# Linear attention and a gated feed-forward in one kernel: the first q tile is loaded and normalised alone, by head halves, and the last output tile is made by columns

## The chip, the cores and the metric

The kernel runs on one core of a Trainium2 chip. The metric is the device time of one execution in microseconds, the median over several runs. The core has a matrix engine (TensorE; PE in the profile, with its weight loads as PEld), a vector engine (VectorE, DVE), a scalar engine (ScalarE, ACT), GpSimd (POOL) and SyncE (SP). SP computes nothing here; it issues most of the DMAs. Each engine works through its own list of instructions in order, and semaphores hold an instruction back until what it needs is there.

## The reference

Eight batches of eight heads, with 576 positions and 64 channels a head, go through linear attention with a cosine weighting. The result is regrouped to 4608 tokens of 512 channels, normalised by its root mean square, and sent through a gated feed-forward of width 1536.

```python
theta = np.pi / 2.0 * pos / S
phi = lambda x: concat([relu(x) * cos(theta), relu(x) * sin(theta)])      # 64 -> 128 channels
kv  = einsum('bhsf,bhsd->bhfd', phi(k), v)          # 128 x 64 for each head
z   = sum over s of phi(k)
num = einsum('bhsf,bhfd->bhsd', phi(q), kv);  den = phi(q) . z + 1e-06
x   = (num / den)  as  [B * S, H * D] = [4608, 512]
xn  = x / sqrt(mean(x * x) + 1e-06) * rms_g
out = (silu(xn @ w_gate) * (xn @ w_val)) @ w_out    # 512 -> 1536 -> 512
```

Inputs and output are float32. The kernel multiplies in bfloat16 and accumulates in float32.

## The kernel before

**Tiles.** The 576 positions of a batch are four tiles of 128 (number c or j; position 4p + j lies on partition p) and a tail of 64. The tails of two batches make one more tile of 128, so there are nine feed-forward blocks of 512 tokens: one for each batch, and block 8 from the eight tails.

**From q, k, v to a token tile.** `k_phi` and `q_phi` make one half each (cosine or sine) of phi for one tile, on DVE or ACT. `v_cast` brings v to bfloat16. `kvz_pe` (in the opening `kvz_half`) multiplies phi(k) and v for each head, 5 matmuls a head, and v carries a column of ones, so z comes along; `kvz_evac` copies the result out of PSUM. phi(q) has to be transposed: in batches 0 and 1 by PE (`q_tr_pe`, then a copy `q_tr_evac`), later by a DMA on SP's queue (`q_tr_dma`). `nd_pe` multiplies it with kv, one matmul a head, and `nd_post` divides by the denominator on DVE (three instructions: add, reciprocal, multiply). `x_sq` takes the sum of squares on ACT and the power of -1/2 on POOL (`rs`), `x_norm` scales on DVE with `gb`, the norm's weights, and the tile is transposed again: `x_tr_pe` and `x_tr_evac` in batches 0 and 1, `x_tr_dma` on SP's queue later.

**The feed-forward.** A block has 12 steps n. `gval_step` makes the gate and the value of 128 hidden channels for 512 tokens (four matmuls of 512 columns into psG, four into psV), then silu on ACT and the product on DVE. Four `out_step`s follow, one for each tile j, of 12 matmuls each, with a copy out of PSUM and a store.

**What sets the order.** The list of every engine is written out by hand. After batch 0, the work on the next batches is put into slots: `at(block, n, where, ...)` hangs it to step n of a block (12 to 15 are the four `out_step`s), `pe` ahead of the step's matmuls, `pre` after them and ahead of silu or the store, `post` at the end. In the opening, block 0 is made in pieces by `open_ffn` as its token tiles come (steps 0 to 5; 128 or 256 columns at a time), and `filler` puts matmuls on zeros between them. The second layer of block 0 (`out_mm`, lines 712 to 737) goes step by step through n for all four tiles at once, with the work of batch 1 in between.

**Queues.** SP issues loads, transposes and stores in program order. Its DMAs use eight semaphores in turn, so each also waits until the eighth before it has landed. POOL issues the weights, which are converted to bfloat16 on the way: `gval_slice` makes one DMA each for w_gate (wg) and w_val (wv), for hidden channels 0 to 256, 256 to 768 and 768 to 1536. The first of them waits for the first half of v. Steps 0 and 1 need the first pair, steps 2 to 5 the second, steps 6 to 11 the third. The loads of batch 1 on SP wait for the third wg (line 614), and the four DMAs of w_out (wo, three steps n each) on POOL wait for q of batch 1 (line 627). The q tails, with batch 2 behind them, wait for the third quarter of wo (line 723).

**The opening's loads on SP** (lines 121 to 137): k heads 0 to 3, k heads 4 to 7, tiles 0 and 1 of q (one DMA), v heads 0 to 3, 4 and 5, 6 and 7, tiles 2 and 3 of q, `gb`. ACT issues the tails of k and v.

Of the kernel before, what the change touches and what calls it, by code (L numbers as in the profile page):

```python
# [9 lines left out]
FP32 = mybir.dt.float32  # L10
# [12 lines left out]
def kernel(  # L23
# [37 lines left out]
    psO = ps_open.tile([P, 2, 512], FP32, name="psO")  # L61

# [44 lines left out]
    def load_pair(which, b, jj, queue=nc.sync, heads=(0, 8)):  # L107

        key = (which, b)
        if key not in raw:  # L110
            raw[key] = one.tile([P, H, 4 * D], FP32, name=f"r{which}", tag=f"r{which}")
        view = src_of[which][b, :, 0:512, :].rearrange("h (p j) d -> p h j d", j=4)
        return queue.dma_start(
            out=raw[key][:, heads[0] : heads[1], jj * 2 * D : (jj + 1) * 2 * D],
            in_=view[:, heads[0] : heads[1], 2 * jj : 2 * jj + 2, :].rearrange(
                "p h j d -> p h (j d)"
            ),
        )
# [6 lines left out]
    load_pair("q", 0, 0)  # L125
    first["v"] = load_main("v", v, 0, LOW)
    load_main("v", v, 0, (4, 6))
    load_main("v", v, 0, (6, 8))
    load_pair("q", 0, 1)
# [213 lines left out]

    x_of = {}
    state = {"x": 0}
    rs_of = {}

    def nd_post(b, j, pst):
        o = headview(pst)
        xt = xts[state["x"] % NXT]  # L350
        state["x"] += 1
        rec = four.tile([P, 2, 4], FP32, name="rec", tag="rec")
        nc.vector.tensor_scalar(
            out=rec[:, :, :], in0=o[:, :, :, D], scalar1=1e-6, scalar2=None, op0=ALU.add
        )
        nc.vector.reciprocal(out=rec[:, :, :], in_=rec[:, :, :])
        nc.vector.tensor_tensor(  # L357
            out=xt[:, 0:DM].rearrange("p (b h d) -> p b h d", b=2, d=D),
            in0=o[:, :, :, 0:D],
            in1=rec[:, :, :].unsqueeze(3).to_broadcast([P, 2, 4, D]),  # L360
            op=ALU.mult,
        )
        x_of[(b, j)] = xt
# [100 lines left out]
    pairs = [(psG[0], psV[0]), (psG[1], psV[1]), (psO, psO)]  # L464
    filler(26, idle)
# [8 lines left out]
    def gval_slice(c0, c1):  # L474
# [5 lines left out]
        weight_dmas[0].ins, first["v"].ins.name, SYNC_DEP, reason="weights after v"  # L480
# [3 lines left out]
    for c in (0, 1):  # L484
        q_phi(V, 0, c, 0)
        q_phi(A, 0, c, 1)
    for c in (0, 1):
        bank = (psG[1] if c == 0 else psV[1])[:, :]
        q_tr_pe(0, c, bank)
        filler(3, idle)  # L490
        q_tr_evac(V, 0, c, bank)
    v_cast(A, 0, LOW)
    v_cast_tail(A, 0)
    filler(2, idle)
# [4 lines left out]
    filler(1, idle)  # L499
    v_cast(V, 0, (4, 6))  # L500
    v_cast(V, 0, (6, 7))
    v_cast(A, 0, (7, 8))
    kvz_half(0, half_view[1], range(4, 6))
    filler(1, idle)
    kvz_half(0, half_view[1], range(6, 8))
    filler(2, idle)
    kvz_half_evac(A, 0, half_view[0], 0)
    kvz_half_evac(V, 0, half_view[1], 1)
    for c in (2, 3):
        q_phi(A, 0, c, 1)  # L510
    nd_pe(0, 0, psA)
    nd_pe(0, 1, psO)
    nd_post(0, 0, psA)
    x_sq(0, 0)
    nd_post(0, 1, psO)
    x_sq(0, 1)
    filler(10, idle)
    q_phi(V, 0, 2, 0)
    x_norm(0, 0)
    q_phi(V, 0, 3, 0)  # L520

    def open_ffn(pair, steps, c0, c1, base=0):

        x = xnT[0]
        for i, n in enumerate(steps):
            for a, w in ((0, wg), (1, wv)):
                bank = pairs[pair][a]
                bank = bank[:, a, :] if pair == 2 else bank[:, :]
                lo = base + 256 * i + c0 % 256
                for t in range(NDT):  # L530
                    nc.tensor.matmul(  # L531
                        bank[:, lo : lo + c1 - c0],
                        lhsT=w[:, t, n * P : (n + 1) * P], rhs=x[:, t, c0:c1],
                        start=(t == 0), stop=(t == NDT - 1),
                    )

    def open_h(pair, n, half):
        if 0 not in hTs:
            hTs[0] = two.tile([P, NNT, TB], BF16, name="hT", tag="hT")
        g, v_ = (  # L540
            pairs[pair][a][:, a, :] if pair == 2 else pairs[pair][a][:, :] for a in range(2)
        )
# [9 lines left out]
    q_tr_pe(0, 2, psO[:, 0, :])  # L552
    q_tr_evac(A, 0, 2, psO[:, 0, :])
    x_tr_pe(0, 0, psG[1][:, :])
    x_tr_evac(V, 0, 0, psG[1][:, :])
    x_norm(0, 1)
    filler(1, idle)
    open_ffn(0, (0, 1), 0, 128)
    x_tr_pe(0, 1, psG[1][:, :])
    x_tr_evac(V, 0, 1, psG[1][:, :])  # L560
    q_tr_pe(0, 3, psO[:, 1, :])
    q_tr_evac(A, 0, 3, psO[:, 1, :])
    nd_pe(0, 2, psA)
    nd_post(0, 2, psA)
    open_ffn(0, (0, 1), 128, 256)
    nd_pe(0, 3, psA)
    nd_post(0, 3, psA)
    x_sq(0, 2)
    open_ffn(1, (2, 3), 0, 256)
# [40 lines left out]
    wo_dmas = []  # L610

    def first_loads_of_1():
        d = load_main("k", k, 1, bufs=two)
        tc.add_manual_dep(d.ins, weight_dmas[4].ins.name, SYNC_DEP, reason="after the weights")
        load_tail("k", k, 1)
        gate = load_main("q", q, 1)
        load_main("v", v, 1, LOW)
        load_main("v", v, 1, HIGH)
        load_tail("v", v, 1)
        for i in range(4):  # L620
            d = nc.gpsimd.dma_start(
                out=wo[:, 3 * i : 3 * i + 3, :],
                in_=moe_w_out[3 * i * P : 3 * (i + 1) * P, :].rearrange("(t p) m -> p t m", p=P),
            )
            wo_dmas.append(d)
            if i == 0:
                tc.add_manual_dep(d.ins, gate.ins.name, SYNC_DEP, reason="after batch 1")

    first_loads_of_1()


    for c in range(5):
        at(0, 7 + c // 3, "post", k_phi, V, 1, c, 0)
        at(0, 7 + c // 3, "post", k_phi, A, 1, c, 1)
    for c in range(4):
        at(0, 9 + c // 2, "post", q_phi, V, 1, c, 0)
        at(0, 9 + c // 2, "post", q_phi, A, 1, c, 1)
    at(0, 11, "post", v_cast, A, 1, LOW)
    at(0, 11, "post", v_cast, V, 1, HIGH)
# [3 lines left out]
    for nb in range(2, B):  # L643
# [10 lines left out]
        vb, vn = (b, 2) if late else (b - 1, 14)  # L654
# [7 lines left out]
        for j in range(4):  # L662
            n = nds[j]
            at(b, n, "pe", nd_pe, nb, j, psA)
            at(b, n, "pre", nd_post, nb, j, psA)
            at(b, n, "post", x_sq, nb, j)
            at(b, n + 1, "post", x_norm, nb, j)
            at(b, n + 1, "post", x_tr_dma, nb, j)
# [38 lines left out]
    def tr1(j):  # L707
        x_tr_pe(1, j, psV[j % 2][:, :])
        x_tr_evac(A, 1, j, psV[j % 2][:, :])

    qbank = [psA[:, 0, :], psV[0][:, :], psV[1][:, :], psA[:, 0, :]]
    for n in range(NNT):
        for c in ((0, 1), (2,), (3,))[n] if n < 3 else ():
            q_tr_pe(1, c, qbank[c])
            q_tr_evac(V if c % 2 else A, 1, c, qbank[c])
        if n == 3:
# [10 lines left out]
        if n in (7, 9, 11):  # L727
            x_norm(1, n // 2 - 3)
        if n in (4, 6, 8, 10):
            j = n // 2 - 2  # L730
# [3 lines left out]
        if n in (9, 11):  # L734
            tr1(n // 2 - 4)
        for j in (2, 3, 0, 1) if n == NNT - 1 else range(4):
            out_mm(0, j, n, banks0[j])
    out_store(A, 0, 2, banks0[2])
    out_store(V, 0, 3, banks0[3])
    tr1(2)  # L740
# [3 lines left out]
    for n in range(2):  # L744
        gval_mm(1, n, n, (0, 256))
    x_tr_pe(1, 3, psC[0][:, :])
    x_tr_evac(A, 1, 3, psC[0][:, :])
# [16 lines left out]
    for blk in range(1, 9):  # L764
        for n in range(2 if blk == 1 else 0, NNT):
            gval_step(blk, n)
        for j in range(4):
            out_step(blk, j)

# [29 lines left out]
```

## Time and profile before

| | |
|---|---|
| median of 6 runs | 337.5 us (335.79 to 339.81) |
| profiled execution: its time, its span | 338.65 us, 336.9 us |
| PE busy | 321.7 us, 96% of the span |
| of it on zeros (`filler`, 49 matmuls) | 13.7 us |
| DVE, ACT busy | 180.6 us, 169.5 us |
| first feed-forward matmul | at 20.21 us |
| step 6 of block 0, first `out_mm` | at 32.92 us, at 45.00 us |
| first matmul of block 2 | at 100.22 us |
| last copy out of PSUM begins | at 332.24 us |

Times inside an execution count from the first instruction. The span ends with the last instruction; 1.75 us of the execution's time lie around it. PE is the engine with the most work, so what counts is where it waits, where it works on zeros, and what it waits for. A wait is put down to the engine or the DMA whose signal came last.

### The profile page before, as it was taken

The numbers are of one execution on the slowest core, as the hardware profiler recorded it, in microseconds if no ns is written. First come the engines' busy times: TensorE is split into PE (matmuls) and PEld (weight loads), VectorE is DVE, ScalarE is ACT, GpSimd is POOL, SyncE is SP. The second block draws the span as 40 slices with busy tenths as digits, with TensorE's granted clock in tenths as the row PEclk, the third lists the DMA queues.
The fourth block names the chain that finished last, engine by engine and source line by source line (L and its number), as shares of the span: only waits on it lengthen the run. The fifth ranks groups of instructions, "written<-read, shape, count | busy, mean of one in ns | idle before, by whom it ended". The sixth has DMA issues, their size and how long they took to land.

```text
span 336.9 us, 5945 instructions
## 1 busy us (share of the span) xinstructions
PE 321.7 (96%) x2193; PEld 163.3 (48%) x2193; DVE 180.6 (54%) x372; ACT 169.5 (50%) x327; POOL 37.5 (11%) x83
## 2 busy tenths in 40 slices
PE   8789999899959999999999999999999999999994
PEld 3569455544424544454455445544544444444441
DVE  3675747577824676467446764674567334203410
ACT  5655853775625456644564566455654233223321
POOL 3520311101100012001100120011001000000000
PEclk9999999999998999999999999999999999999999
DMA  8999999968696977797769678877552310030014
GB/s 206 283 207 264 275 187 254 328 152 191 151 248 129 199 180 201 180 205 178 221 152 219 166 215 157 204 191 226 126 74 44 105 54 0 2 120 5 2 31 94
DMA packets 94957, 54.14 MB, mean 161 GB/s; under 512 B 59984, under 2 KB 90192, under 8 KB 94928
## 3 DMA queue, kind: packets, MB, share of 16 engines
q1 hardware_dynamic: 89072, 48.78, 57.6%
q0 software_dynamic: 4768, 4.72, 8.5%
q10 hardware_dynamic: 1088, 0.26, 0.4%
q8 instruction: 17, 0.28, 0.4%
q14 instruction: 12, 0.10, 0.1%
HBM read 38.01 MB, written 9.44 MB: 141 GB/s over the span
## 4 chain that ended last, share of the span: by engine, by line
PE 81%; DMA 9%; SPq 3%; DVE 2%; ACT 2%; issue 1%; POOL 0%; DVEq 0%; ACTq 0%
PE psC L440 24%; PE psG L420 24%; PE psV L420 24%; DMA rq<-in_q_dram 6%; PE psA L303 2%; PE psA L331 2%; SPq L86 2%; DMA wo<-in_moe_w_out_dram 2%; DMA out_dram<-osb 1%; PE psG L460 1%; DVE xt L357 1%; PE psG L531 1%; PE psV L531 1%; PE psO L531 1%; SPq L75 1%
## 5 line engine op out<-in xcount | busy, mean ns | idle before, releaser
L435 DVE TENSOR_TENSOR hT<-psV,sg 128x512 bf16<-128x512 f32 x102 | 70.4, 690 | 103.9 <-PE psV L420 90.4
L420 PE MATMUL psG<-xnT,wg 128*128 128x512 bf16 (+1 forms) x368 | 93.6, 377 | 4.9 <-DMA rq<-in_q_dram 3.5
L429 ACT ACTIVATE sg<-psG 128x512 f32<-128x512 f32 x102 | 60.6, 594 | 69.1 <-PE psG L420 69.0
L420 PE MATMUL psV<-xnT,wv 128*128 128x512 bf16 (+1 forms) x368 | 93.6, 377 | 0.0
L440 PE MATMUL psC<-wo,hT 128*128 128x512 bf16 x408 | 92.0, 379 | 0.7 <-DMA wo<-in_moe_w_out_dram 0.7
L440 PEld LDWEIGHTS <-hT 128*128 128x128 bf16 x432 | 41.2, 98 | 48.5 <-DMA wo<-in_moe_w_out_dram 0.8
L420 PEld LDWEIGHTS <-wv 128*128 128x128 bf16 x416 | 40.9, 98 | 48.0 <-issue 1.1
L420 PEld LDWEIGHTS <-wg 128*128 128x128 bf16 x416 | 38.9, 98 | 46.1 <-issue 6.5
L275 ACT COPY osb<-psC 128x512 f32<-128x512 f32 x33 | 19.3, 586 | 46.4 <-PE psC L440 46.4
L374 POOL TENSOR_TENSOR rs<-ms,mhalf 128x1 f32<-128x1 f32 x36 | 19.9, 554 | 202.4 <-ACT scr L369 202.4
L369 ACT ACTIVATE scr<-xt 128x513 bf16<-128x513 f32 x36 | 22.9, 635 | 25.9 <-DVE xt L357 25.1
L381 DVE SCALAR_TENSOR_TENSOR xn<-xt,rs,gb 128x512 bf16<-128x512 f32 x36 | 27.3, 757 | 15.2 <-POOL rs L374 15.2
L357 DVE TENSOR_TENSOR xt<-psA,rec 128x512 f32<-128x512 f32 x35 | 24.2, 691 | 1.2
L216 ACT ACTIVATE qp<-rq,tab 128x512 bf16<-128x512 f32 x32 | 22.2, 713 | 1.7 <-DMA rq<-in_q_dram 1.7
L216 ACT ACTIVATE kpm<-rk,tab 128x512 bf16<-128x512 f32 (+1 forms) x34 | 21.2, 675 | 0.4 <-DMA rk<-in_k_dram 0.4
L218 DVE TENSOR_SCALAR kpm<-rk,tab 128x512 bf16<-128x512 f32 (+1 forms) x38 | 15.2, 451 | 4.1 <-ACT tab L171 3.1
L331 PEld LDWEIGHTS <-qpT 128*128 128x128 bf16 x256 | 12.2, 98 | 7.8 <-issue 0.6
L218 DVE TENSOR_SCALAR qp<-rq,tab 128x512 bf16<-128x512 f32 x32 | 15.2, 487 | 0.6 <-DMA rq<-in_q_dram 0.6
L460 PE MATMUL psG<-warm 128*128 128x512 bf16 x49 | 13.7, 424 | 1.2 <-DVE fidx L153 1.2
L331 PE MATMUL psA<-kvzs,qpT 128*128 128x65 bf16 x248 | 13.1, 193 | 0.4 <-DVE xt L357 0.3
L420 PE MATMUL psG<-xnt_tail,wg 128*128 128x512 bf16 x48 | 12.3, 379 | 0.0
L420 PE MATMUL psV<-xnt_tail,wv 128*128 128x512 bf16 x48 | 12.3, 379 | 0.0
(90 smaller groups left out, 189.9 us busy)
## 6 DMA issues: line engine op xcount, KB each, us to landing
out_dram<-osb SPq DMA_DIRECT2D x32, 256.0 KB, 2.8
rv<-in_v_dram SPq DMA_DIRECT2D x22, 256.0 KB, 3.2
rk<-in_k_dram SPq DMA_DIRECT2D x20, 256.0 KB, 3.4
rq<-in_q_dram SPq DMA_DIRECT2D x20, 256.0 KB, 3.2
rk<-in_k_dram SPq DMA_DIRECT2D x2, 1024.0 KB, 7.7
rq<-in_q_dram SPq DMA_DIRECT2D x2, 1024.0 KB, 8.6
rv<-in_v_dram SPq DMA_DIRECT2D x3, 512.0 KB, 9.2
wo<-in_moe_w_out_dram POOLq DMA_DIRECT2D x4, 384.0 KB, 7.4
```

The costliest lines, as they stand in the source:

```text
L216: nc.scalar.activation(out=out_ap, in_=in_ap, func=AF.Relu, scale=scale)
L218: eng.tensor_scalar(out=out_ap, in0=in_ap, scalar1=scale, scalar2=0.0, op0=ALU.mult, op1=ALU.max)
L275: nc.scalar.copy(out=o, in_=i)
L331: nc.tensor.matmul(o[:, g, i, :], lhsT=qpT[(b, 0)][:, h, j * P : (j + 1) * P], rhs=kvzs[(b, g)][:, i * E : (i + 1) * E], start=True, stop= ...
L357: nc.vector.tensor_tensor(out=xt[:, 0:DM].rearrange("p (b h d) -> p b h d", b=2, d=D), in0=o[:, :, :, 0:D], in1=rec[:, :, :].unsqueeze(3). ...
L369: nc.scalar.activation(out=scr[:, :], in_=xt[:, 0 : DM + 1], func=AF.Square, scale=1.0 / math.sqrt(DM), accum_out=ms[:, :],)
L374: nc.gpsimd.tensor_tensor(out=rs[:, :], in0=ms[:, :], in1=mhalf[:, :], op=ALU.pow)
L381: nc.vector.scalar_tensor_tensor(out=xn[:, :], in0=x_of[(b, j)][:, 0:DM], scalar=rs_of[(b, j)][:, :], in1=gb[:, :], op0=ALU.mult, op1=ALU. ...
L420: nc.tensor.matmul(pst[bank][:, cols[0] : cols[1]], lhsT=w[:, t, n * P : (n + 1) * P], rhs=x[:, t, cols[0] : cols[1]], start=(t == 0), sto ...
L429: nc.scalar.activation(out=sg[:, :], in_=psG[bank][:, :], func=AF.Silu)
L435: nc.vector.tensor_tensor(out=hTs[blk][:, n, :], in0=psV[bank][:, :], in1=sg[:, :], op=ALU.mult)
L440: nc.tensor.matmul(bank, lhsT=hTs[blk][:, n, j * P : (j + 1) * P], rhs=wo[:, n, :], start=(n == 0), stop=(n == NNT - 1),)
```

## The change

The first q load brings tile 0 alone, then v, then tile 1 alone, and tiles 2 and 3 together. The first weight DMA waits for that first q load in place of the first half of v. The first quarter of wo is issued on POOL right behind the weights; the other three wait for the first half of v of batch 1 in place of q.

In the opening, tile 0 of q is transposed alone. Its `nd_pe` and `nd_post` are done by head halves, each in its own bank (psO is now two tiles). Tile 1 follows after it. `open_ffn` for steps 2 and 3 now runs in two pieces of 128 columns, the first right behind that of steps 0 and 1 and ahead of tile 1's transposes; before, it ran once with 256 columns behind `nd_pe(0, 3)`. ACT and DVE share the copies in another way, and there are 43 fillers for 49.

In block 0, phi of batch 1 sits one step later, and its last q tile and its cast of v move into the second layer. Batch 1's tiles sit at steps 4, 6, 8, 9 of it for 4, 6, 8, 10, and its last two steps are done pair by pair. In block 1 the cast of batch 2's v sits one step earlier. `x_norm` and `x_tr_dma` in slots 12 and later go to `pre`, ahead of that step's store. The last tile of block 8 is made in two halves of 256 columns in two banks, each copied and stored by itself, by SP and ACT.

```diff
-    load_pair("q", 0, 0)
-    first["v"] = load_main("v", v, 0, LOW)
+    first["q"] = load_tokens("q", 0, 0, 1)
+    load_main("v", v, 0, LOW)
     load_main("v", v, 0, (4, 6))
     load_main("v", v, 0, (6, 8))
-    load_pair("q", 0, 1)
+    load_tokens("q", 0, 1, 2)
+    load_tokens("q", 0, 2, 4)
...
-        weight_dmas[0].ins, first["v"].ins.name, SYNC_DEP, reason="weights after v"
+        weight_dmas[0].ins, first["q"].ins.name, SYNC_DEP, reason="weights after q"
...
+    wo_load(0)
+    q_phi(V, 0, 0, 0)
+    q_phi(A, 0, 0, 1)
+    q_tr_pe(0, 0, psV[0][:, :])
+    q_tr_evac(V, 0, 0, psV[0][:, :])
+    filler(4, idle)
+    v_cast(A, 0, (0, 2))
+    v_cast(V, 0, (2, 4))
+    v_cast_tail(V, 0)
...
+    q_phi(V, 0, 1, 0)
+    nd_half(0, 0, 0, psO[0])
+    nd_post_half(0, 0, 0, psO[0])
+    q_phi(A, 0, 1, 1)
+    nd_half(0, 0, 1, psO[1])
+    nd_post_half(0, 0, 1, psO[1])
+    x_sq(0, 0)
...
     q_phi(V, 0, 2, 0)
     x_norm(0, 0)
+    q_tr_pe(0, 2, psO[0][:, :])
+    filler(2, idle)
+    nd_post(0, 1, psA)
     q_phi(V, 0, 3, 0)
...
     x_tr_pe(0, 0, psG[1][:, :])
-    x_tr_evac(V, 0, 0, psG[1][:, :])
-    x_norm(0, 1)
+    x_tr_evac(A, 0, 0, psG[1][:, :])
+    x_sq(0, 1)
+    q_tr_evac(A, 0, 2, psO[0][:, :])
     filler(1, idle)
     open_ffn(0, (0, 1), 0, 128)
...
+    q_tr_pe(0, 3, psO[1][:, :])
+    q_tr_evac(A, 0, 3, psO[1][:, :])
+    x_norm(0, 1)
+    open_ffn(1, (2, 3), 0, 128)
+    x_tr_pe(0, 1, psA[:, 0, :])
+    x_tr_evac(V, 0, 1, psA[:, 0, :])
     nd_pe(0, 2, psA)
     nd_post(0, 2, psA)
     open_ffn(0, (0, 1), 128, 256)
+    open_ffn(1, (2, 3), 128, 256)
     nd_pe(0, 3, psA)
     nd_post(0, 3, psA)
     x_sq(0, 2)
-    open_ffn(1, (2, 3), 0, 256)
...
+    gate = load_main("v", v, 1, LOW)
+    load_main("v", v, 1, HIGH)
+    load_tail("v", v, 1)
+    d = wo_load(1)
+    tc.add_manual_dep(d.ins, gate.ins.name, SYNC_DEP, reason="after batch 1")
...
-        vb, vn = (b, 2) if late else (b - 1, 14)
+        vb, vn = (b, 1) if late else (b - 1, 14)
...
-            at(b, n + 1, "post", x_norm, nb, j)
-            at(b, n + 1, "post", x_tr_dma, nb, j)
+            where = "pre" if n + 1 >= NNT else "post"
+            at(b, n + 1, where, x_norm, nb, j)
+            at(b, n + 1, where, x_tr_dma, nb, j)
...
-        for j in range(4):
+        for j in range(4 if blk < 8 else 3):
             out_step(blk, j)
+    for half, bank in ((0, psC[1]), (1, psG[0])):
+        c = slice(256 * half, 256 * half + 256)
+        for n in range(NNT):
+            nc.tensor.matmul(
+                bank[:, 0:256], lhsT=hTs[8][:, n, 3 * P : 4 * P], rhs=wo[:, n, c],
+                start=(n == 0), stop=(n == NNT - 1),
+            )
+        copy(A, osb[:, c], bank[:, 0:256])
+        for i in range(2):
+            r0 = (6 + i) * S + 512
+            (nc.sync if i == 0 else A).dma_start(
+                out=out[r0 : r0 + 64, c], in_=osb[64 * i : 64 * i + 64, c]
+            )
```

## The prediction

> **What bounds the kernel now.** I read the chain of waits first, then PE's waits, then the busy time by stage, and at last the timelines of PE and SP where a stage shows a wait. The page's part 4 gives the chain that ended last:
>
> ```profile
> PE 81%; DMA 9%; SPq 3%; DVE 2%; ACT 2%; issue 1%; POOL 0%; DVEq 0%; ACTq 0%
> ```
>
> So PE sets the end, and only what takes PE's idle or filler time away counts. These are PE's waits between 60 and 104 us (total, times, longest), and after them two stages (busy PE, PEld, DVE, ACT, POOL, then granted clock, DMA share, GB/s):
>
> ```profile
> PE psG L420 <- DMA rq<-in_q_dram: 3.5, 1, 3.5
> PE psA L303 <- DVE vvm L277: 0.8, 1, 0.8
> PE psG L420 <- ACT osb L275: 0.7, 1, 0.7
> PE psG L420 <- ACT xnT L275: 0.7, 1, 0.7
> ...
> 96.70:100.20 3.50, 0.01 (x1) 0.00 (x0) 0.53 (x1) 0.58 (x1) 0.00 (x0) 1.00 1.11 255
> 100.20:103.90 3.70, 3.68 (x10) 1.37 (x10) 0.23 (x1) 1.21 (x2) 0.00 (x0) 0.54 0.68 164
> ```
>
> Ahead of block 2 PE stands still for 3.5 us and then works at a clock of 0.54, which costs another 3.7 x 0.46 = 1.7 us. From 104 us to the last matmul PE waits for nothing, so the change can win only in the opening, in block 0's second layer, in block 1, and in the tail.
>
> **The opening: what arrives when.** Two DMA views, of 13 to 14.2 us and of 15 to 16 us, and issues with their median us to landing:
>
> ```profile
> q1 hardware_dynamic: 523, 0.37, 117.1%
> ...
> q0 software_dynamic: 397, 0.20, 145.9%
> ...
> wg<-in_moe_w_gate_dram POOLq DMA_DIRECT2D x1, 512.0 KB, 7.8
> wv<-in_moe_w_val_dram POOLq DMA_DIRECT2D x1, 512.0 KB, 9.6
> ```
>
> SP's loads are q1, POOL's weights q0. The first weight DMA is issued at 11.83 us, yet up to 14.2 us only SP's queue moves anything, and from 15 on only the weights do. The engines are full in both windows. So the weights start when SP's loads have passed, not when they are issued. Issuing them 2.9 us sooner (q's load landed at 1.79 + 7.9 = 9.7 us and now lands by about 8.7, v's first half at 2.34 + 9.2 = 11.5) changes the order of transfers at most, not their sum. The second wv, issued at 14.31, landed at 23.9 and will land close to that again.
>
> Tile 0 itself comes sooner. Its q load has half the bytes of the old pair, which took 2.5 us behind k (7.2 to 9.7): 1.25 us by bytes, 2.5 by its unchanged number of pieces; I take 1.5, so it and the v loads behind it come 1.0 us sooner, v's last quarter at 12.0 for 13.0. From there: cast 0.6, two heads of kv and their copy 1.3 (0.38 of it the copy), half an `nd_pe` 0.3, two half `nd_post` on DVE 1.3 behind that (a whole one took 1.13, 15.79 to 16.92), `x_sq` 0.8, POOL 0.65, `x_norm` 0.75, transposes 0.45, copy on ACT 0.65. That is 18.8 us for the first feed-forward matmul, against 20.21. The `filler`s cover these waits and cost nothing by themselves; nor does going from 49 to 43 gain.
>
> **The opening: what PE then does.** This is PE before, its first feed-forward matmuls and its first use of the second wv (start, us):
>
> ```profile
> 20.21 0.38 PE L531 MATMUL psG<-xnT,wg 128*128 128x128 bf16 x4 [0.37 <-DVE xnT L277]
> ...
> 24.10 0.60 PE L531 MATMUL psV<-xnT,wv 128*128 128x256 bf16 x4
> ```
>
> It uses that weight 0.2 us after its landing, and does tile 1's transposes and both `nd_pe` of tiles 2 and 3 ahead of it. The changed order has only 1.55 us of work ahead of it: 16 matmuls of 128 columns (0.88, from 20.21 to 21.11), eight transposes (0.45), four matmuls (0.22). PE gets there at about 21 and waits until 24. Tile 1's transposes and the `nd_pe` of tiles 2 and 3 are queued behind the waiting matmul, and DVE, ACT and POOL wait for those in turn.
>
> From 20.21 to step 6 at 32.92 PE had 12.7 us less one wait of 0.33, so 12.4 of work; 12.4 - 1.55 = 10.8 remain. From 24.0 that ends at 34.8. Three waits come on top. `nd_pe(0, 2)` needs psA, which now holds tile 1's transposes until DVE has copied them (0.16 + 0.42): 0.6. Tile 2's transposes need `x_norm(0, 2)`, which on DVE stands behind `nd_post(0, 3)`: that `nd_pe` comes at 27.6, the division ends at 29.1, the norm at 29.8, and PE is there at 28.6: 1.2. Block 0's silu and products then run one behind the other: 0.3. Step 6 starts at about 36.7, 3.8 us later than before. I take the weight at 23.8, so 3.6. Lower bound: were the second wv there in time, the same replay from 18.8 gives 33.6, 0.7 later than before, since the `nd_pe` of tiles 2 and 3 now come behind four pieces of feed-forward.
>
> **wo.** Before, the first `out_mm` waited 0.7 us for wo; now that quarter is there: -0.7. It delays nothing that PE waits for: the third wv, landed at 31.5 and used at 33.8, lies ahead of it. Quarters 1 to 3 are issued at about 41 to 43 for 40 to 41.5 and needed from 51 on.
>
> **Block 0's second layer.** Same matmuls. Of the two 0.7 us waits, one was for the copy out of psG[0]. In the new order that copy stands on ACT behind `x_sq(1, 3)` and a transposes' copy, and ends about 0.8 us after PE wants the bank. The other, for tile 3's copy, has `out_store(A, 0, 0)` ahead of it on ACT as before. So 0, between -1.4 (both gone) and +0.6.
>
> **Block 1.** The earlier cast of v removes 0.8 us of waiting for vvm. But SP's timeline decides what follows (start, us):
>
> ```profile
> 87.54 2.84 SPq L86 DMA_DIRECT2D rvt<-in_v_dram  x2
> ...
> 94.47 0.48 SPq L450 DMA_DIRECT2D out_dram<-osb  x1
> 95.05 1.20 SPq L400 DMA_TRANSPOSE xnT<-xn  x1
> ```
>
> SP issues from 70.94 to 101 with no real pause, and the transpose that block 2 needs is issued at 95.05 and lands 5.1 us later, while its `x_norm` was done at 91.1. PE's earlier end of block 1 only makes the wait longer. What shortens it is the one store that the transpose now passes (0.6). Against that, DVE does both v casts ahead of the first `q_phi`, with only 0.44 idle there: SP's stretch begins 0.3 later. Net -0.4. The half clock stays likely, since the wait is then 3.5 + 0.8 - 0.3 = 4.0 us; without it -1.7.
>
> A rule speaks here: by the Trainium skill ("TensorE: Matmul & The Clock Gate", Part 1) the clock is halved after one idle window of about 3.4 us that runs freely. The rows agree once (3.5 us idle, then 0.54), and by the rule a wait under 3.4 us would save the 1.7.
>
> **Later blocks.** `x_norm` and its transpose in `pre`: PE waits for neither there; 0.
>
> **Tail.** The last copy took 0.58 for 512 columns, then SP issued two stores, 0.5 apart, each landing 2.4 us on. With 256 columns the copy is about 0.38 (the 128x260 copy on ACT), and the two stores go out side by side, ACT's issue taking 0.2 longer than SP's: -0.2 - 0.5 + 0.2 = -0.5, bounds -0.2 and -0.9. I take -0.6, for the smaller stores. The 24 matmuls of 256 columns cost what 12 of 512 did.
>
> **Sum**: 3.6 - 0.7 + 0 - 0.4 - 0.6 = +1.9 us. The profiled execution took 338.65 (span 336.9 and 1.75 around it), so 340.55. It was 1.15 above the median of 337.5; against that the forecast is **339.4 us**.
>
> **Rivals.**
> 1. *Slower, 345 us*: the weights, now issued while 1.3 MB of SP's loads are still waiting, get turns between them. At 310 GB/s those take 4.1 us from 11.3 on; with a third of the engines' time, 12.3, and `gb`, last in the queue, lands at 24 instead of 15.5. `x_norm(0, 0)` waits for it; the first feed-forward matmul comes 1.9 later, at 26, and the second weight matmul 3.6 later than forecast. PE idles for a whole window and runs at half clock: 1.7 more. It decides from `gb` later than 20.5 (24.0 - 1.55 - 1.9); below that the wait for wv hides it. For it: only the issue order kept them apart before. Against it: in 12 to 14.2 us the weights, though issued, got nothing.
> 2. *Faster, 334 us*: the transfers overlap with a gain and the second wv comes by 21.5, so 0.7 for 3.6; SP isn't stopped at the two v tails (2.84; 1.29 at 122.76): -1.5, and the clock stays up, if the wait ahead of block 2 goes under 3 us. Against it: full engines in both DMA windows.
> 3. *The earlier weights do nothing and PE hides more than I replay* (the change does not do what it says): 337 to 338.
>
> By the Trainium skill ("DMA: Bandwidth & Descriptors", Queues, rings and completion order) each DMA engine takes turns between its queues packet by packet. That is rival 1's mechanism and speaks against this change; the rows of 12 to 16 us show one queue after the other, no turns. By the rule in its fine form `gb` lands near 20, and the sum stays 339.4.
>
> **Numbers.** Forecast 0.46, rival 1 0.2, rival 2 0.19, rival 3 0.15. The forecast's own range is 337.5 to 341.5. Half of rival 1 lies above 345 and half of rival 2 below 334; to leave out no more than 2 in 10 the range goes from **334** to **345**. A measurement of this kernel tells about 1% from no change (334.1 and 340.9): faster 0.15 (rival 2, but for its upper quarter), slower 0.33 (rival 1 and the forecast's upper quarter), same 0.52.
>
> **What would show it.** Right: first feed-forward matmul near 19, PE waiting 2 to 3 us for the second wv, step 6 at 36 to 37, no wait for wo, block 2 still waiting 3 us or more for its last transpose, 4 us from PE's last matmul to the end. Wrong: weights and SP's loads in the same DMA window between 11 and 15 us; the second wv landing by 22; `x_norm(0, 0)` waiting for `gb`; a clock of 0.5 before 30 us.

## The result, and the profile after

The changed kernel takes 339.45 us (median of 29 runs, 337.33 to 342.93), the kernel before 337.64 us in the 64 runs beside them. The ratio, which leaves out the two slowest of the 29 runs, is 1.0074, with a 95% interval of 1.0056 to 1.0092: slower by a little under 1%. (It isn't the quotient of the two medians, 1.0054.) The forecast was 339.4 us. That it agrees to 0.1 us is luck: errors of the sum cancel, as the stages show. Both profiled executions, in us:

| | before | after | change | forecast |
|---|---|---|---|---|
| execution, its span | 338.65, 336.88 | 339.57, 337.56 | span +0.68 | +1.9 |
| first feed-forward matmul | 20.21 | 20.20 | 0 | -1.4 |
| from there to step 6 | 12.71 | 18.64 | +5.93 | +5.0 |
| step 6 to the first `out_mm` | 12.08 | 11.25 | -0.83 | -0.7 |
| first `out_mm` to block 2 | 55.22 | 53.15 | -2.07 | -0.4 |
| block 2 to the last matmul | 231.98 | 230.32 | -1.66 | 0 |
| last matmul to the end | 4.68 | 4.00 | -0.68 | -0.6 |

So the opening is 5.9 us slower, not 3.6, and everything behind it is 5.2 us faster, not 1.7. These are PE's waits from 20 to 45 us in the changed kernel (total, times, longest), and below them, from the same kernel, those from 60 to 110 us:

```profile
PE psV L570 <- DMA wv<-in_moe_w_val_dram: 2.1, 1, 2.1
PE psA L431 <- DVE xn L406: 1.0, 1, 1.0
PE psG L570 <- DMA wg<-in_moe_w_gate_dram: 0.6, 1, 0.6
PE psA L329 <- DVE xnT L275: 0.5, 1, 0.5
```

```profile
PE psG L445 <- DMA xnT<-xn: 1.7, 1, 1.7
PE psA L329 <- DMA qpT<-qp: 0.9, 1, 0.9
PE psG L445 <- ACT xnT L273: 0.7, 1, 0.7
PE psG L445 <- ACT osb L273: 0.3, 1, 0.3
```

The first list is what was added: PE stands for the second w_val, before that for the second w_gate, and later for the transposes' copy and for a norm, as the replay had it. The second list is what was won: the wait ahead of block 2 is 1.7 us for 3.5, the wait for v's cast (vvm) is gone, and a wait of 0.9 for a transposed phi(q) (qpT) has come in its place.

PE's timeline, and then two stretches with their busy times (PE, PEld, DVE, ACT, POOL), the granted clock, the DMA share and GB/s, show the opening's stall and what follows it:

```profile
22.29 0.40 PE L570 MATMUL psG<-xnT,wg 128*128 128x128 bf16 x4 [0.59 <-DMA wg<-in_moe_w_gate_dram]
24.79 0.40 PE L570 MATMUL psV<-xnT,wv 128*128 128x128 bf16 x4 [2.11 <-DMA wv<-in_moe_w_val_dram]
25.03 0.39 PE L570 MATMUL psG<-xnT,wg 128*128 128x128 bf16 x4
...
27.24 0.63 PE L570 MATMUL psV<-xnT,wv 128*128 128x128 bf16 x4
27.67 0.63 PE L570 MATMUL psG<-xnT,wg 128*128 128x128 bf16 x4
```

```profile
22.27:25.68 3.41, 1.28 (x20) 1.12 (x21) 0.10 (x1) 0.49 (x1) 0.00 (x0) 1.00 1.19 211
25.68:29.10 3.42, 2.90 (x34) 2.75 (x32) 1.49 (x4) 0.72 (x2) 0.00 (x1) 0.50 1.16 209
```

The four matmuls at 24.79 start 0.24 us ahead of the next four, those at 27.24 start 0.43 ahead. In between the clock was halved, for 3.42 us. PE was busy for 2.90 of them, so at most 1.45 us were lost; fill_wait, below, shows 1.3. That is a cost which the forecast had put into a rival only. Before, such a stretch lay behind the wait ahead of block 2 (100.2 to 103.9 us, shown above). In the changed kernel the clock stays up there, which is the whole of the -1.66 in the table.

One load explains a part of the first row of the table. The timelines of POOL and DVE show what the first norm waits for in the changed kernel, and below, the same norm before:

```profile
17.17 0.57 POOL L399 TENSOR_TENSOR rs<-ms,mhalf 128x1 f32<-128x1 f32 x1 [1.89 <-ACT scr L394]
18.32 0.75 DVE L406 SCALAR_TENSOR_TENSOR xn<-xt,rs,gb 128x512 bf16<-128x512 f32 x1 [1.06 <-DMA gb<-in_moe_rms_g_dram]
```

```profile
18.42 0.75 DVE L381 SCALAR_TENSOR_TENSOR xn<-xt,rs,gb 128x512 bf16<-128x512 f32 x1
```

`gb` landed at 18.19 us, where it had landed at 15.48. SP's queue has one load more ahead of it: its issue starts at 9.90 us, behind the landing of q's first tile at 9.53 (the eighth DMA before it, if ACT's four loads of the tails are counted too), and lasts 2.70; before, it started at 7.92 and lasted 1.90. By then the weights are moving too. So the tile that was brought forward is normalised at 18.32 us, where it had been at 18.42. Without `gb` it could have been at 17.73, when `rs` was done: 0.6 of DVE's wait of 1.06 us is due to `gb` alone.

### The profile page after: what moved, and what is told of

Its sections match the earlier page's. It is cut to its first block, busy times and chain, and to the rows that moved or that the text cites. A ratio compares the mean times of both kernels' runs of the same rounds, so it can differ in the third digit from the quotient of the medians.

```text
span 337.6 us, 6000 instructions
## 1 busy us (share of the span) xinstructions
PE 321.3 (95%) x2215; PEld 164.8 (49%) x2215; DVE 181.0 (54%) x375; ACT 169.5 (50%) x328; POOL 37.9 (11%) x83
## 4 chain that ended last, share of the span: by engine, by line
PE 83%; DMA 8%; ACT 3%; DVE 3%; POOL 1%; issue 1%; SPq 0%; ACTq 0%; DVEq 0%
PE psG L445 25%; PE psV L445 25%; PE psC L465 22%; DMA wv<-in_moe_w_val_dram 4%; PE psA L329 2%; DMA rq<-in_q_dram 2%; PE psA L301 2%; DMA xnT<-xn 1%; PE psV L570 1%; PE psG L570 1%; DMA qpT<-qp 1%; PE psG L465 1%; DVE xt L383 1%; PE psO L570 1%; DVE xn L406 1%
## 5 line engine op out<-in xcount | busy, mean ns | idle before, releaser
L465 PE MATMUL psC<-wo,hT 128*128 128x512 bf16 x396 | 89.3, 379 | 0.0
L465 PEld LDWEIGHTS <-hT 128*128 128x128 bf16 x420 | 40.2, 98 | 46.4
L273 ACT COPY osb<-psC 128x512 f32<-128x512 f32 (+1 forms) x33 | 19.1, 580 | 44.8 <-PE psC L465 44.1
L216 DVE TENSOR_SCALAR kpm<-rk,tab 128x512 bf16<-128x512 f32 (+1 forms) x38 | 15.9, 469 | 4.5 <-DMA rk<-in_k_dram 4.5
L485 PE MATMUL psG<-warm 128*128 128x512 bf16 x43 | 12.6, 434 | 1.2 <-DVE fidx L151 1.2
```

The lines of the kernel that those rows point to most:

```text
L216: eng.tensor_scalar(out=out_ap, in0=in_ap, scalar1=scale, scalar2=0.0, op0=ALU.mult, op1=ALU.max)
L273: nc.scalar.copy(out=o, in_=i)
L465: nc.tensor.matmul(bank, lhsT=hTs[blk][:, n, j * P : (j + 1) * P], rhs=wo[:, n, :], start=(n == 0), stop=(n == NNT - 1),)
```

## The experiments

Eleven kernels, run in three sets, each set beside the kernel before (its median was 337.55, 336.50 and 336.84 us in the three: old_opening to ffn23_back and gate_v; fill_wait, gb_early, q_pair and slots_back; the last three). The changed kernel has a fourth set, that of the result. As the kernel before moves by 1 us, kernels of different sets are compared by their ratios to it; 0.001 is 0.34 us. In the stage table that follows, "half" counts the stretches of 3.41 us at half clock up to the last matmul of the profiled execution. The executions of one kernel differ in it, which the last section takes up, so medians and stages are read together.

| kernel | median us (runs) | ratio to before (95% interval) | first FFN matmul | step 6 | first `out_mm` | wait ahead of block 2 | block 2 to last matmul | half |
|---|---|---|---|---|---|---|---|---|
| before | 337.64 (64) | | 20.21 | 32.92 | 45.00 | 3.5 | 231.98 | 1 |
| after | 339.45 (29) | 1.0074 (1.0056 to 1.0092) | 20.20 | 38.84 | 50.09 | 1.7 | 230.32 | 1 |
| old_opening | 334.92 (12) | 0.9926 (0.9895 to 0.9957) | 20.28 | 32.98 | 44.24 | 2.7 | 232.01 | 1 |
| new_opening | 342.92 (6) | 1.0158 (1.0103 to 1.0213) | 19.74 | 40.17 | 51.43 | 2.9 | 231.98 | 3 |
| ffn23_back | 335.39 (12) | 0.9953 (0.9923 to 0.9983) | 19.86 | 34.15 | 45.40 | 2.0 | 230.33 | 0 |
| fill_wait | 337.88 (12) | 1.0036 (1.0007 to 1.0066) | 19.74 | 37.00 | 48.26 | 1.8 | 230.33 | 0 |
| gate_v | 340.94 (6) | 1.0115 (1.007 to 1.016) | 19.31 | 39.99 | 51.24 | 1.6 | 230.33 | 2 |
| gb_early | 339.40 (12) | 1.0094 (1.0057 to 1.0131) | 20.61 | 37.72 | 48.97 | 1.5 | 230.32 | 0 |
| q_pair | 339.42 (12) | 1.0059 (1.002 to 1.0099) | 19.26 | 39.05 | 50.31 | 1.4 | 230.32 | 2 |
| slots_back | 341.62 (11) | 1.0121 (1.0084 to 1.0157) | 19.85 | 40.14 | 51.39 | 2.2 | 232.02 | 3 |
| tail_only | 335.14 (12) | 0.9963 (0.9929 to 0.9996) | 20.31 | 33.02 | 45.59 | 3.2 | 232.01 | 1 |
| fill_block2 | 333.73 (9) | 0.9930 (0.9898 to 0.9962) | 20.20 | 32.98 | 44.23 | (filled) | 230.33 | 0 |
| v3_on_pool | 332.34 (6) | 0.9873 (0.9838 to 0.9908) | 20.19 | 32.98 | 44.23 | none | 230.33 | 0 |

### The two halves of the change

**old_opening**: the changed kernel with the whole opening of before. In its core:

```
-    first["q"] = load_tokens("q", 0, 0, 1)
-    load_main("v", v, 0, LOW)
+    load_pair("q", 0, 0)
+    first["v"] = load_main("v", v, 0, LOW)
...
-    load_tokens("q", 0, 1, 2)
-    load_tokens("q", 0, 2, 4)
+    load_pair("q", 0, 1)
...
-        weight_dmas[0].ins, first["q"].ins.name, SYNC_DEP, reason="weights after q"
+        weight_dmas[0].ins, first["v"].ins.name, SYNC_DEP, reason="weights after v"
...
+    open_ffn(1, (2, 3), 0, 256)
```

> The changed kernel with the whole opening of before (loads, gate of the weights, order up to step 6), everything behind it as changed, the early quarter of wo too. Theory A (the loss lies in the opening, and what was edited behind it gains by itself): step 6 at 32.9 us again, no wait for wo, the wait ahead of block 2 under 2 us and no half clock behind it, about 333.5 us. Rival B (the wait ahead of block 2 was only shorter because block 1 began 5 us later, while transfers went on): the wait is back at 3.5 us with the half clock, and only wo (0.7) and the tail (0.6) are left of the gain, 336 to 336.5 us.

**new_opening**: the kernel before with the same pieces the other way round, and nothing of what lies behind step 6.

```
-    load_pair("q", 0, 0)
-    first["v"] = load_main("v", v, 0, LOW)
+    first["q"] = load_tokens("q", 0, 0, 1)
+    load_main("v", v, 0, LOW)
...
+    open_ffn(1, (2, 3), 0, 128)
...
+    open_ffn(1, (2, 3), 128, 256)
```

> The kernel before with the opening of the changed one, nothing else. Theory A: step 6 at about 38.8 us, 5.9 later; the wait ahead of block 2 stays at 3.5 us with its half clock; 343 us. Rival B: the later start shortens that wait to under 2 us; 339 to 340 us.

Measured: 334.92 and 342.92 us. With before and after, that makes a square. By the ratios, the new opening costs 1.58%, or 5.3 us, with the rest as before, and 1.0074 - 0.9926 = 1.48%, or 5.0 us, with the rest as changed; what lies behind it brings 0.74%, or 2.5 us, with the old opening and 0.84%, or 2.8 us, with the new one. Theory A holds for where the loss lies. For the wait ahead of block 2 neither theory was right, and the square says how the two share it. PE's longest wait between 60 and 104 us, first in old_opening, then (60 to 112 us) in new_opening:

```profile
PE psG L447 <- DMA xnT<-xn: 2.7, 1, 2.7
```

```profile
PE psG L445 <- DMA rq<-in_q_dram: 2.9, 1, 2.9
```

From 3.5 us, the edits alone take 0.8 (to 2.7), the late start alone takes 0.6 (to 2.9), both take 1.8 (to 1.7). (These are single executions: tail_only, which is the kernel before up to there, had 3.2.) A late opening thus got back some of what it lost, at a wait that had nothing to do with it.

### What in the opening costs the time

**ffn23_back**: only the feed-forward of steps 2 and 3 moves back.

```
-    open_ffn(1, (2, 3), 0, 128)
...
-    open_ffn(1, (2, 3), 128, 256)
...
     x_sq(0, 2)
+    open_ffn(1, (2, 3), 0, 256)
```

> The changed kernel with the feed-forward of steps 2 and 3 for tiles 0 and 1 in one piece of 256 columns behind the last nd_pe, as before; all else as changed. Theory A (PE stands before the second wv with work queued behind): the wait for wv falls under 0.5 us, no half clock in the opening, step 6 at 34.5 to 35.5 us, 335 to 336 us. Rival C (PE would then wait for DVE, ACT and POOL just as long, since x_norm comes late with gb): step 6 at 37.5 or later, 338 us or more.

Measured: 335.39 us, 4.1 less than the changed kernel. Step 6 starts at 34.15 us for 38.84. In PE's waits from 14 to 45 us the weights no longer stand; the longest are these:

```profile
PE psA L431 <- DVE xn L406: 0.7, 1, 0.7
PE psG L431 <- DVE xn L406: 0.6, 1, 0.6
PE psA L329 <- DVE xnT L275: 0.5, 1, 0.5
```

Rival C falls: the norms come 0.7 us late at the most. One group of matmuls, put in front of work that was ready, on a weight that was not, was most of the opening's loss. No run splits the 1.2 us that are left of it (34.15 for 32.92), nor tries the head halves or the fillers of the opening by themselves.

**fill_wait**: the order stays, but PE gets something to do while it stands.

```
+                if pair == 1 and n == 2 and a == 0 and c0 == 0:
+                    filler(9, psA[:, 0, :])
```

> The changed kernel with nine matmuls on zeros (1.95 us) between the gate and the value part of step 2, where PE stood 2.1 us for the second wv; nothing waits for them. Theory E (the clock goes down after a stretch of 3.41 us in which PE was busy for less than about half; the wait itself stays): wait for wv 0.2 us, no half clock before 30 us, step 6 at 37.1 us (38.84 less 1.7), about 1.5 us less than the changed kernel in the median, 338 us. Rival F (the waits cause the loss by themselves and the half clock is not a matter of filling): 339.5 us, half clock between 25 and 30 us as before.

Measured: 337.88 us, 1.6 less than the changed kernel in the medians and 1.3 by the ratios (1.0036 for 1.0074), by matmuls on zeros. The timeline of PE:

```profile
21.97 2.11 PE L485 MATMUL psA<-warm 128*128 128x512 bf16 x9
24.24 0.40 PE L570 MATMUL psV<-xnT,wv 128*128 128x128 bf16 x4 [0.16 <-DMA wv<-in_moe_w_val_dram]
```

The second w_val landed at 24.20 and was used at 24.24; step 6 came at 37.00, with no half clock anywhere in the execution up to the tail. Theory E holds: all twelve runs have a mean clock of 0.997 or more, three of the changed kernel's 29 have. The loss of the opening splits thereby: 37.00 - 32.92 = 4.1 us are order and transfers. Of the 1.8 us that the changed kernel loses on top, the second w_val, 0.55 us later, is one part, the half clock the other: from the first matmul with that weight to step 6 it took 14.05 us for 12.76, so 1.3.

### The transfers

**gate_v**: the first weight DMA waits for v's first half again.

```
-        weight_dmas[0].ins, first["q"].ins.name, SYNC_DEP, reason="weights after q"
+        weight_dmas[0].ins, first["v"].ins.name, SYNC_DEP, reason="weights after v"
```

> The changed kernel with the first weight DMA waiting for the first half of v again. Theory A (the weights begin to move when SP's loads run dry, whatever their issue; gb is late because one more load stands ahead of it in SP's queue): gb lands at 17.5 us or later and the second wv at 24.5 or later; 339.5 us, no difference. Rival D (the weights issued early take gb's turns): gb lands by 16.5 us, the first feed-forward matmul at 18.8, 338 us or less.

Measured: 340.94 us; `gb` landed at 17.07 us, the second w_val at 25.62. Theory A named `gb` at 17.5 or later and missed by 0.4; Rival D named 16.5 or earlier, and 338 us or less, and missed by more. The weights' first packet came at 14.9 us here (issued at 11.25), at 14.5 in the changed kernel (issued at 9.83), at 14.4 before (issued at 11.83): issued 1.4 us sooner, they start 0.4 us sooner. So their start hangs little on their issue, as the forecast had it. Their arrival hangs on it more: the second w_val landed 0.9 us sooner in the changed kernel than here and `gb` 1.1 us later (0.7 to 0.8 later in the four other kernels with these loads and this order of them), so the early weights do seem to take some of its turns. The times, 1.0115 for 1.0074, have intervals that overlap; that the gate is worth something in the end is not shown.

**gb_early**: `gb` is loaded ahead of q's tile 1.

```
     load_main("v", v, 0, (6, 8))
+    gb = one.tile([P, DM], FP32, name="gb")
...
     load_tokens("q", 0, 1, 2)
     load_tokens("q", 0, 2, 4)
-    gb = one.tile([P, DM], FP32, name="gb")
```

> The changed kernel with the load of gb ahead of that of q tile 1 in SP's queue, nothing else. Theory A (the late gb sets the first feed-forward matmul, but not the end of the opening, since PE then stands for the second wv): gb lands by 15 us, x_norm of tile 0 starts at 17.5 to 17.8, the first feed-forward matmul at 19.0 to 19.4; the wait for wv grows by as much; step 6 within 0.5 us of 38.8, more idle time and so more half clock, 339.5 to 341 us. Rival G (gb is what made the tile come late and the opening with it): step 6 1 us sooner, 338 us.

Measured: 339.40 us. `gb` landed at 13.34, yet the norm of tile 0 did not come sooner (first feed-forward matmul at 20.61), which neither theory had. DVE's timeline says why:

```profile
17.89 0.49 DVE L216 TENSOR_SCALAR qp<-rq,tab 128x512 bf16<-128x512 f32 x1 [0.80 <-DMA rq<-in_q_dram]
18.29 0.75 DVE L406 SCALAR_TENSOR_TENSOR xn<-xt,rs,gb 128x512 bf16<-128x512 f32 x1
```

On DVE `q_phi` of tile 2 stands ahead of the norm, and it waits for the third q load, which now is the last in SP's queue and landed at 17.86. Whichever load comes last takes its place in the chain. Step 6 came 1.1 us sooner, as Rival G had it, but in an execution without a half clock; nine of the twelve runs have a mean clock of 0.994 or less, and the time shows no gain. The DMA view of the same kernel from 14 to 16 us shows why the last one is so late:

```profile
q0 software_dynamic: 393, 0.20, 72.3%
q1 hardware_dynamic: 462, 0.24, 56.8%
```

The weights (q0) and SP's loads (q1) share the engines about evenly, packet counts and bytes alike. That is the mechanism of the forecast's rival 1, here with 0.24 MB of SP's loads in the way of the weights instead of all of them. By the Trainium skill ("DMA: Bandwidth & Descriptors", Queues, rings and completion order) a DMA engine takes turns between its queues packet by packet; this view agrees. The two windows that the forecast showed of the kernel before had one queue each; between them, from 14.35 us (first packet of the weights) to 14.89 (last of SP's), both moved there too.

**q_pair**: tiles 0 and 1 of q come in one load again, all else as changed.

```
-    first["q"] = load_tokens("q", 0, 0, 1)
+    first["q"] = load_tokens("q", 0, 0, 2)
...
-    load_tokens("q", 0, 1, 2)
```

> The changed kernel with q tiles 0 and 1 in one load at the place of tile 0's, so 512-byte pieces as before and one load less in SP's queue. Theory H (the two loads of 256-byte pieces moved 255 KB per us against 310, and cost the weights 0.8 us): the second wv lands at 23.9 to 24.1, gb by 16; step 6 at about 38 us; 338.5 us. Rival I (the weights' transfer time differs from run to run and not by the pieces): wv lands at 24.5 or later; 339.5 us.

Measured: `gb` at 15.55 us, the second w_val at 23.62, 1.1 us sooner than in the changed kernel and a little sooner than Theory H named: Theory H by its transfers. In the profiled executions of the seven kernels with tiles alone that weight landed at 24.20 to 25.62, in those of the six with the pair at 23.62 to 24.10. The DMA view from 12 to 13.5 us, of the changed kernel and then of q_pair (packets, MB, share):

```profile
q1 hardware_dynamic: 1129, 0.38, 126.9%
```

```profile
q1 hardware_dynamic: 862, 0.46, 117.9%
```

With tiles alone the engines needed 1129 packets for 0.38 MB and were as full as with 862 packets for 0.46 MB. But step 6 came at 39.05 us, not at 38, and the time was 339.42 us, that of the changed kernel: PE came to the weight at 21.5 for 22.7 us and stood for the same 2.1, and its profiled execution has two stretches at half clock where the changed kernel's has one. Of transfers that come 1.1 us sooner, nothing is left in the median behind this order; the ratio, 1.0059 for 1.0074, leaves room for half a us.

### Behind the opening

**slots_back**: the casts of v of batch 2, and the norms and transposes, are put back into their old slots.

```
-        vb, vn = (b, 1) if late else (b - 1, 14)
+        vb, vn = (b, 2) if late else (b - 1, 14)
...
-            where = "pre" if n + 1 >= NNT else "post"
+            where = "post"
```

> The changed kernel with the casts of v of batch 2 one step later and the norms and transposes behind the stores again, both as before; all else as changed. Theory A (these two edits shortened the wait ahead of block 2): a wait for vvm of 0.8 us again, the wait ahead of block 2 at 2.5 us or more, with a half clock behind it; 341 to 342 us. Rival B (the wait is short because block 1 starts late): the wait stays under 2 us; 339.5 to 340.3 us.

Measured: 341.62 us, 2.2 more than the changed kernel in the medians, 1.6 by the ratios (1.0121 for 1.0074). The wait for vvm is back (0.8), the wait ahead of block 2 is 2.2 us, between the two theories' numbers, and a half clock lies behind it (block 2 to the last matmul 232.02 us). The two edits were worth about 0.8 + 0.5 by the waits, and 1.7 where the clock held.

**tail_only**: the kernel before with the last tile by columns, as in the change.

```
-        for j in range(4):
+        for j in range(4 if blk < 8 else 3):
             out_step(blk, j)
...
+    for half, bank in ((0, psC[1]), (1, psG[0])):
```

> The kernel before with the last tile by columns, nothing else. Theory A: from PE's last matmul to the end 4.0 to 4.1 us for 4.7, no other stage changes; 0.6 us less than before in the stage, too little for the medians to tell surely (ratio 0.998, interval across 1). Rival J (24 matmuls of 256 columns cost more than 12 of 512, each with its own weight load): the last tile takes 0.3 us or more longer, and the gain is half of that.

Measured: 335.14 us, ratio 0.9963 (0.9929 to 0.9996). From the last matmul to the end it took 3.72 us (332.36 to 336.08) for 4.68, a little more than expected, and the 24 matmuls cost nothing extra (last matmul at 332.36 for 332.20, with block 2 0.13 later). Theory A, and Rival J falls.

**fill_block2** and **v3_on_pool** start from old_opening, the better kernel by then. The first puts zeros into the wait ahead of block 2, the second takes out what the wait was put down to: six loads in SP's queue.

```
+            if blk == 2 and n == 0:
+                filler(8, psC[0][:, :])
```

> The changed kernel with the opening of before (as in the run of that name, 334.92 us), and eight matmuls on zeros (1.73 us) at the start of block 2, where PE stands 2.7 us for the last transpose. Theory E (the clock goes down after a stretch of 3.41 us with PE busy under about 0.45): the wait falls to about 1 us, block 2 starts at 98.2 us as before, no half clock behind it; 333.3 to 334.0 us, and a narrower spread. Rival F (the clock depends on the wait for the transpose or on something else than PE's busy share): half clock at 98 to 102 us, 335 us.

```
     def load_piece(which, b, p):
+        queue = nc.gpsimd if (which, b) == ("v", 3) else nc.sync
...
+                queue=queue,
...
-            load_tail(which, src_of[which], b)
+            load_tail(which, src_of[which], b, queue)
```

> The changed kernel with the opening of before, and v of batch 3 (six loads, 3.6 us of SP's time between 79 and 90 us) issued by POOL in place of SP. Theory K (SP's issue time sets when the last transpose ahead of block 2 starts): the transpose is issued at 91 to 92 us for 93.70, the wait ahead of block 2 under 1.2 us, no half clock; 332.0 to 333.3 us. Rival L (the transfers set it, since the DMA engines are full and the transposes take 4 us to land whenever they are issued; or POOL's powers for the norms come late behind the loads): the wait stays at 2 us or more, 334.5 to 335.5 us.

Measured: 333.73 us, and 332.34 us, the fastest of all, 1.3% below the kernel before. In PE's timeline, of fill_block2 and then of v3_on_pool, block 2 starts behind the zeros and behind the last `out_step`:

```profile
96.12 1.89 PE L487 MATMUL psC<-warm 128*128 128x512 bf16 x8
97.85 1.03 PE L447 MATMUL psG<-xnT,wg 128*128 128x512 bf16 x4
```

```profile
90.42 5.35 PE L469 MATMUL psC<-wo,hT 128*128 128x512 bf16 x24
95.61 1.03 PE L449 MATMUL psG<-xnT,wg 128*128 128x512 bf16 x4
```

Theory E holds again in this execution: four matmuls of 512 columns in 1.03, full clock, where old_opening's took 1.61 behind its wait:

```profile
98.22 1.61 PE L447 MATMUL psG<-xnT,wg 128*128 128x512 bf16 x4 [2.68 <-DMA xnT<-xn]
```

But the ratio of fill_block2, 0.9930, is that of old_opening, 0.9926, and four of its nine runs have a mean clock of 0.992 or 0.993, as a stretch at half clock leaves it; where it lies in them the record doesn't show. So a gain in time by these zeros is not shown. SP's timeline, in old_opening and then in v3_on_pool, has the last transpose ahead of block 2:

```profile
93.70 1.29 SPq L427 DMA_TRANSPOSE xnT<-xn  x1
```

```profile
90.23 1.27 SPq L429 DMA_TRANSPOSE xnT<-xn  x1
```

In v3_on_pool it lands at 94.41, ahead of PE's need. Theory K holds, and more than it said: no wait is left, where under 1.2 us had been expected. Against old_opening that is 0.5%, or 1.8 us (0.9873 for 0.9926).

## Why the prediction was right, and where it was not

**What bounds the kernel**: right. PE waits for nothing behind block 2 in any of the runs; that stretch takes 230.3 us, and 1.7 more where it begins at half clock.

**The opening, the arrivals**: half right. The weights' start was set by SP's loads and hardly by their issue (9.83 for 11.83 us, 2.0 sooner and not 2.9), though their arrival followed the issue in part (gate_v). But the forecast said that the change alters the order of transfers at most, not their sum: the two loads of one tile alone, in more packets, cost the second w_val 1.1 us (24.75 for 23.62 in q_pair), more than the early issue brought, so it came 0.8 later than before. The first feed-forward matmul was put at 18.8 and came at 20.20. Two terms failed. The forecast had q's tile 0 and v's last quarter 1.0 us sooner, and they landed 0.2 and 0.1 sooner (9.53 for 9.71, 12.97 for 13.04; the other kernels with these loads have v's at 12.51 to 12.65); `rs` was done at 17.73, where the sum has 16.95. The other term is `gb`: the step costed the tile's own chain and left out the last load in the queue, which the forecast had only in rival 1, and there at 24.0 us. It landed at 18.19 and cost 0.6 more.

**The opening, what PE does**: right in mechanism and in most of its size. PE stood for the second w_val with tile 1 queued behind it (2.1 us, after 0.6 for w_gate; 2 to 3 had been named), and ffn23_back shows that this order is most of the loss. From that weight to step 6 the forecast had 12.7 us (24.0 to 36.7); fill_wait, without half clock, took 12.8 (24.24 to 37.00). The mis-sized term is the clock: the sum had none for the opening, and by the rule that the forecast cites a wait of 3 us is no whole idle window. It took 1.3 us in the profiled execution. With it, and the weight 0.95 us later than taken, 3.6 becomes 5.9, which is what was measured.

**wo**: right, -0.83 for -0.7, with no wait for it. The early quarter does this by itself in old_opening (11.25 us from step 6 to the first `out_mm`); in new_opening, without it, the late start does it (11.25 too).

**Block 0's second layer**: -0.43 (15.55 to 15.12 us from the first `out_mm` to block 1) for 0, within its bounds.

**Block 1**: the mechanism was right (SP's issue sets the last transpose, shown by v3_on_pool), the size was not: -1.64 for -0.4, which with the layer makes the -2.07 of the table. The step set 0.8 us of waiting against a wait that would grow by as much, and missed that PE's later start shortens this wait too (0.6 in new_opening). The half clock behind it was named as likely, with -1.7 without it; it was without it.

**Tail**: right, -0.68 for -0.6.

**The sum**: +5.93 - 0.83 - 2.07 - 1.66 - 0.68 = +0.69 us between two profiled executions, where +1.9 was forecast. The median moved by 1.8 all the same. The forecast took the profiled execution's 1.15 us above the median for something that both kernels have; the changed kernel's lies 0.12 above its own. The clock doesn't explain that. In the three sets the kernel before has 28 of 77 runs with the mean clock of one stretch at half clock (0.992 to 0.995), as its profiled execution has (0.994); their median is 337.48 us, 1.2 below it, and why is open. The changed kernel's runs with such a clock have a median of 339.14, so at an equal clock it is 1.7 us slower; where neither shows a stretch (0.996 or more) it is 337.48 for 335.44 us, 2.0 slower.

**The rivals**: rival 1 (turns between the queues, `gb` late) happened in its mechanism, weakly, and `gb` came 2.3 us ahead of the point from which it decides. Rival 2's clock that stays up came true behind block 1, its early weight did not. Rival 3 fell.

**The signs**: of the six that were to show the forecast right, three came (2.1 us of waiting for the second w_val, none for wo, 4.0 us at the end); the first feed-forward matmul (20.20), step 6 (38.84) and the wait ahead of block 2 (1.7) lay elsewhere. Of the four that were to show it wrong, three came too: the weights and SP's loads in one window (from 14.52 us on), the norm that waits for `gb`, and a half clock before 30 us. That the number held is luck; that PE's order is the main cause of the loss is not, as ffn23_back shows.

## What to carry to other kernels

Before you bring a tile forward, look at the load that comes last in its queue and at every instruction ahead of the tile's own on its engine: the chain waits for those, and moving one load only changes which one it is. Never put a matmul whose weight is still under way ahead of work that is ready, since the engine keeps its order: that cost 4 us here, whatever arrived sooner. And judge a change by stages in more than one execution: a late start can win back time at an old wait further on, and this is no merit of the change; the better repair was to take that wait away at its cause, the queue that issued too much.

## What the runs showed of the hardware

**When the clock goes down.** The granted clock changes only at points 3.41 us apart, whose place differs from execution to execution. I took the stretches between these points in all thirteen profiled executions, from the first row of the clock to the last matmul. Behind a stretch at full clock the next one was at half clock wherever PE had been busy for 1.51 us of 3.41 or less (a share of 0.44), and at full clock wherever it had been busy for 1.61 or more (0.47). Behind a stretch at half clock, where the same work takes longer, it stayed down up to a share of 0.74 and was up again from 0.85 on. No wait has to fill the stretch. The highest share with half clock after it is from gate_v, the lowest without from fill_wait (the columns are those of the stretches above):

```profile
19.47:22.88 3.41, 1.51 (x24) 1.16 (x21) 0.89 (x2) 1.98 (x4) 0.55 (x1) 1.00 1.24 204
22.88:26.29 3.41, 1.23 (x11) 0.97 (x12) 0.00 (x0) 0.52 (x1) 0.00 (x0) 0.50 1.18 210
```

```profile
99.16:102.57 3.41, 1.61 (x8) 0.77 (x8) 0.75 (x1) 0.77 (x2) 0.33 (x1) 1.00 1.11 293
```

The Trainium skill ("TensorE: Matmul & The Clock Gate", Part 1) gives the 3.41 us and says that the stretch runs freely, which agrees; its table has the clock halved after an idle stretch, and by that none of the half clocks in the opening would have come. (It also tells of a kernel in which short pauses made the clock go up and down, without a measure of how short or how many.) The waits of 2.7 us (old_opening), 2.9 (new_opening) and 2.2 (slots_back) ahead of block 2 brought it too, those of 2.0 and less did not. The measurement decides: a wait of about 2 us is in danger, and whether it is hit depends on where the points fall. In gb_early a wait of 2.1 us for the second w_val left the two stretches at a share of 0.56 each, and the clock stayed up.

**The spread of the runs.** A stretch at half clock costs 1.7 us at the start of block 2, where PE has work throughout, 1.3 in the opening of the changed kernel, and 0.005 of the mean clock. Of the 29 runs of the changed kernel, three have a mean clock of 0.997 or 0.998 and a median of 337.5 us, thirteen 0.992 to 0.995 and 339.1, eleven 0.988 to 0.990 and 341.1, two 0.985 and 342.8: none, one, two and three such stretches, going by the profiled executions (0.993 with one in the changed kernel, 0.988 with two in gate_v, 0.985 with three in slots_back). With the wait filled, the twelve runs of fill_wait lie within 1.7 us, those of gb_early, with the same waits unfilled, within 3.8.

**Work on zeros can pay** where it keeps the clock up: 1.3 to 1.6 us in fill_wait, for instructions that nothing uses. In fill_block2 it kept the clock up in the profiled execution, and no gain in time is shown.
